# Attention into a squared-ReLU layer on one core: M's tiled matmuls regrouped with the second scores, and the last output tile moved behind tile 34

## The chip, the cores and the metric

The kernel runs on one core of a Trainium2 chip. The metric is device time in microseconds (us) of one execution. Engines are called PE (TensorE, matmuls), DVE (VectorE), ACT (ScalarE), POOL (GpSimd) and SP (SyncE); the last two mostly issue DMAs here. PSUM has eight banks, in which PE leaves its results and from which DVE and ACT copy them out.

## The reference

Eight batches of eight heads, 576 tokens of 64 numbers, and 32 packed queries `p` per head. Two attentions in a row, and then a layer with a squared ReLU over all 4608 tokens:

```python
def sm_attn(qq, kk, vv):
    s = scale * np.matmul(qq, kk.transpose(0, 1, 3, 2))
    s = s - np.max(s, axis=-1, keepdims=True)
    a = np.exp(s)
    a = a / (np.sum(a, axis=-1, keepdims=True) + 1e-09)
    return np.matmul(a, vv)
p_packed = sm_attn(p, k, v)
out = sm_attn(q, p_packed, p_packed)
x = out.transpose(0, 2, 1, 3).reshape(4608, 512)
h = x @ w_in                       # 512 x 2048
r = np.maximum(h, 0.0)
return (r * r) @ w_out             # 2048 x 512
```

## The kernel before, in words

Each batch goes through a chain of steps, and the steps of several batches are woven into one another.

- **Loads.** POOL issues all DMAs for q, k, v and the weights, at most eight in flight, in one order (`Lk`, `Lq`, `Lv`, `LWI` for w_in, `LWO` for w_out).
- **Tk, Tq.** DVE transposes k and q.
- **S1, SX, E.** First scores of `p` against k: PE (`s1`, `s1_both`), maximum on DVE, exponential on ACT, norm on DVE, then PE turns the weights (`s1_tr`) and ACT or DVE copies them out as `e1`.
- **PV, XT.** `pv_both` gives the packed values; `pp_turn` and `spread` on PE and small copies bring them into `ppT` and into the blocks `pq_bd`.
- **S2, C, N.** Second scores of q against the packed values (`s2_both`): 32 matmuls on tiles of 64 x 32 of the array, eight of which run side by side. DVE turns the result out of PSUM (`s2_turn`, three pieces), then maximum, subtraction, exponential (ACT), sum, multiplication and a last turn (`n_turn`) into `a2`.
- **M.** Instead of multiplying the attention weights by the packed values and then by w_in, the kernel first makes M, packed values times w_in: 128 x 2 x 2048 per batch, in four quarters `c` of 512 columns. A quarter is eight matmuls of 64 x 32 tiles with 512 columns (`m`) into two banks. The quarters are copied out either as one wide copy of 1024 columns (`m_out`, where the two banks are a pair) or as two narrow ones (`m_half`).
- **F1.** `f1_mm`: M times `a2`, 16 blocks of 128 rows per batch, each four matmuls of 288 columns into a pair of banks, ReLU on ACT, square on DVE into `gT`.
- **F2.** For each of 36 tiles of 128 tokens, 16 matmuls of 512 columns (`f2_mm`, `gT` times `w_out_b`) into one bank, a copy to `o_sb` and four stores on SP's queue (`store`). The last tile, 35, goes in three pieces of 256, 128 and 128 output columns (`fz_steps`, `fz_mm`), named F2.35, F2.36 and F2.37; each is copied and stored half by SP and half by ACT's queue.

Banks 0 to 3 are the two pairs `HB`, 4 and 5 are `AB`, 6 and 7 are `OB`. F1 takes a pair, F2 a bank of `OB`; scores and M (`mode=2`) take a pair and banks 4 and 5.

The order is made before the program is recorded. `Plan` holds streams of `Step`s; a step has pieces with an engine, a planned duration, banks, and the steps that must be done before it. `forward` goes through planned time and gives each free engine the ready piece with the lowest priority number; the priorities are a base level per kind of step plus the numbers of `TABLE`. A change of `mode` on PE costs `TURN` in the plan. Each engine then works through its own instructions strictly in that order and waits on semaphores. Where the plan leaves PE a gap before the first F2, dummy matmuls on zeros (`keep_clock`) are put in.

The three tiled runs of a batch are these steps before: `S2.b.0` (second scores), `M.b.0` (quarters 0 and 1) and `M.b.2` (quarters 2 and 3):

```python
return [Step(f"M.{b}.{c}", [[[("PE", 0.48, lambda c=c: mm(c))]], outs(c)], [f"XT.{b}/3.0"] + pre(c),
             banks=[x + (4, 5) for x in HB], free=[(1, None)], mode=2) for c in (0, 2)]
```

Of the kernel before, what the change touches and what calls it, by code (L numbers as in the profile page):

```python
# [8 lines left out]
ACT = mybir.ActivationFunctionType  # L9
# [5 lines left out]
P = 128  # L15
# [38 lines left out]
class Plan:  # L54
# [193 lines left out]
TABLE = {'o': {'P.0': -17.44, 'X.0': -515.84, 'P.2': -467.13, 'X.1': -217.88, 'La0': -1045.51, 'La1': -646.79,  # L248
# [47 lines left out]


def kernel_impl(tc, q, k, v, p, w_in, w_out, out):
# [17 lines left out]
    FUSE = ()  # L316
# [3 lines left out]
    with ExitStack() as ctx:  # L320
# [591 lines left out]
        def s1_steps(b):  # L912
            after = [f"X.{min(b // 2, 1)}"] + ([f"PV.{b - 1}.{qd}" for qd in QDS if b == 1 or qd == 0] if b else []) + gate(b, 1)
# [21 lines left out]
        def pv_steps(b):  # L935
# [14 lines left out]
            return [Step(nm, [[[("PE", 0.41, lambda: T[b].pv_both(U[nm]))]]],  # L950
# [9 lines left out]
        def m_steps(b):  # L960
# [19 lines left out]
            def first():  # L980
                T[b].s2_rest(U[f"S2.{b}.1"])
                mm(0)

            def pre(c):
                return [f"LWI.{x}.{i}" for x in (c, c + 1) for i in range(2)] + ([f1n(b - 2, NFB - 1)] if b > 1 else [])
            if b not in FUSE:
                return [Step(f"M.{b}.{c}", [[[("PE", 0.48, lambda c=c: mm(c))]], outs(c)], [f"XT.{b}/3.0"] + pre(c),
                             banks=[x + (4, 5) for x in HB], free=[(1, None)], mode=2) for c in (0, 2)]
            return [Step(f"S2.{b}.1", [NO], [f"XT.{b}"] + [f"Tq.{b}.{qd}" for qd in QDS] + [f"N.{b - 1}.{qd}" for qd in QDS], banks=HB),
                    Step(f"M.{b}.0", [[[("PE", 0.58, first)]]], [f"S2.{b}.1"] + pre(0), banks=[x + (4, 5) for x in HB], mode=2),  # L990
                    Step(f"MX.{b}.0", [NO, outs(0)], [f"M.{b}.0"], free=[(1, f"M.{b}.0")]),
                    Step(f"M.{b}.2", [[[("PE", 0.48, lambda: mm(2))]], outs(2)], [f"XT.{b}/3.0"] + pre(2),
                         banks=[x + (4, 5) for x in HB], free=[(1, None)], mode=2)]

        def m_of(b, fb):
            c = fb * FB // WCH
            return [f"M.{b}.{c}.{x}" for x in QDS] if b in SOLO else [f"{'MX' if b in FUSE and c < 2 else 'M'}.{b}.{c // 2 * 2}"]

        def s2_steps(b):
# [30 lines left out]
            if b in TURNED:  # L1030
                turns = [[("DVE", 0.7 if x == 0 else 0.38, lambda x=x: T[b].s2_turn(x))] for x in range(3)]
                return [Step(nm, [[[("PE", 0.55, lambda: T[b].s2_both(U[nm]))]], turns] + front(4, 1152), pre,
                             banks=[x + (4, 5) for x in HB], free=[(1, None)], mode=2), Step(f"C.{b}", chain(4, 1152), [nm])] + [
                        Step(f"N.{b}.{x}", [[[("DVE", 0.7, lambda x=x: T[b].n_turn(x))]]], [f"C.{b}"] + ([f1n(b - 2, NFB - 1)] if b > 1 else [])) for x in range(2)]
# [175 lines left out]
```

## Time and profile before

| | us |
|---|---|
| median of 3 runs | 250.99 |
| lowest, highest | 250.13, 252.03 |
| the profiled execution | 250.5 |
| its span | 248.7 |
| PE, DVE, ACT, POOL busy in the span | 237.6, 186.9, 168.3, 42.9 |
| granted clock of PE | 0.999 of full |

The span goes from the first to the last instruction that the profiler saw; 1.8 us of the execution's time lie around it. Busy times are sums of the instructions of an engine, and matmuls overlap one another, so the start of one matmul to the start of the next says more than the length of a row. The largest groups are F2 (line 831, 544 matmuls of 512 columns, 138.2 us) and F1 (line 775, 448 matmuls, 70.4 us); M (line 589) has 256 matmuls and the second scores of batches 1 to 7 (line 622) 224. DMA queue 0, which POOL feeds, moves 18.55 MB, and the DMA engines are busy in slices 1 to 16 of 40 and nearly idle afterwards.

### The profile page before, as it was taken

What the parts mean: (1) busy time and instruction counts of PE and PEld (TensorE: products, weight loads), DVE (VectorE), ACT (ScalarE), POOL (GpSimd) and SP (SyncE); (2) the same over time, 40 slices, a digit from 0 to 9 for tenths busy, and PEclk for the clock granted to TensorE, in tenths of its full rate; (3) what the DMA queues carried; (4) which work ended last, traced back from release to release, by engine and by line L of the source; (5) the groups of instructions that cost most, each with busy time, mean ns of one, the idle gap of its engine ahead of it and who ended that gap; (6) DMA issues with size and microseconds to landing.
All of it is one profiled execution on the core that took longest, in us unless ns stands there. A gap on an engine that the chain in (4) does not pass through costs nothing.

```text
span 248.7 us, 5896 instructions
## 1 busy us (share of the span) xinstructions
PE 237.6 (96%) x2352; PEld 130.5 (52%) x2352; DVE 186.9 (75%) x356; ACT 168.3 (68%) x302; POOL 42.9 (17%) x76
## 2 busy tenths in 40 slices
PE   7788899899999999999999999999999999999992
PEld 5464464356534755465536654465444764466641
DVE  5678988997699779956996789946999758765100
ACT  8547899968828868787767855799045883997010
POOL 8745545433334320000000000000000000000000
PEclk9999999999999999999999999999999999999999
DMA  6999999999999999640022103110223101301222
GB/s 111 197 192 207 205 201 203 202 231 240 219 229 221 233 218 221 112 99 22 23 63 65 45 3 83 46 44 3 77 56 81 44 1 42 86 1 42 76 78 60
DMA packets 26715, 28.50 MB, mean 115 GB/s; under 512 B 5440, under 2 KB 18112, under 8 KB 26688
## 3 DMA queue, kind: packets, MB, share of 16 engines
q0 software_dynamic: 18960, 18.55, 45.7%
q1 hardware_dynamic: 6960, 9.32, 13.7%
q8 instruction: 18, 0.29, 0.4%
q10 hardware_dynamic: 768, 0.26, 0.4%
q14 instruction: 9, 0.07, 0.1%
HBM read 37.22 MB, written 9.44 MB: 188 GB/s over the span
## 4 chain that ended last, share of the span: by engine, by line
PE 77%; DMA 16%; POOL 2%; ACT 1%; issue 1%; DVE 0%; DVEq 0%; ACTq 0%; POOLq 0%
PE pb L831 45%; PE ps L775 22%; DMA w_in_b<-in_moe_w_in_dram 8%; DMA w_out_b<-in_moe_w_out_dram 4%; DMA q_b<-in_q_dram 4%; PE ps L589 2%; PE ps L475 2%; PE pb L848 1%; PE pb L500 1%; PE ps L622 1%; PE pb L589 1%; PE pb L514 1%; ACT r L813 1%; POOL k_b L416 0%; POOL q_b L416 0%
## 5 line engine op out<-in xcount | busy, mean ns | idle before, releaser
L831 PE MATMUL pb<-w_out_b,gT 128*128 128x512 bf16 x544 | 138.2, 380 | 0.7 <-DMA w_out_b<-in_moe_w_out_dram 0.6
L831 PEld LDWEIGHTS <-gT 128*128 128x128 bf16 x560 | 51.6, 98 | 59.1 <-issue 8.2
L813 ACT ACTIVATE r<-ps 128x576 bf16<-128x576 f32 x112 | 70.8, 655 | 13.7 <-PE ps L775 10.1
L775 PE MATMUL ps<-a,M 128*128 128x288 bf16 x448 | 70.4, 286 | 0.1
L823 DVE TENSOR_TENSOR gT<-r 128x576 bf16<-128x576 bf16 x112 | 49.7, 455 | 26.5 <-ACT r L813 25.4
L775 PEld LDWEIGHTS <-M 128*128 128x128 bf16 x448 | 42.9, 98 | 20.5 <-issue 1.3
L366 ACT COPY o_sb<-pb 128x512 f32<-128x512 f32 (+1 forms) x18 | 10.3, 571 | 23.8 <-PE pb L831 19.8
L368 DVE COPY o_sb<-pb 128x512 f32<-128x512 f32 (+2 forms) x19 | 12.1, 638 | 14.5 <-PE pb L848 12.8
L487 ACT ACTIVATE e1x<-ps,n 128x576 bf16<-128x576 f32 x16 | 11.8, 743 | 12.9 <-DVE n L483 12.9
L734 ACT ACTIVATE e<-d 128x1152 bf16<-128x1152 f32 (+2 forms) x9 | 9.1, 1008 | 12.9 <-DVE d L729 12.9
L366 ACT CAST M<-pb 128x512 bf16<-128x512 f32 x30 | 16.5, 600 | 1.3 <-PE pb L589 1.3
L366 ACT CAST M<-ps 128x1024 bf16<-128x1024 f32 (+1 forms) x15 | 14.7, 980 | 3.8 <-PE ps L589 3.8
L451 DVE STREAM_TRANSPOSE kT<-k_b 128x576 f32<-128x576 f32 x16 | 12.0, 764 | 2.9 <-DMA k_b<-in_k_dram 2.9
L421 POOL DMA_DIRECT2D v_b<-in_v_dram x16 | 11.2, 700 | 12.9 <-DMA k_b<-in_k_dram 6.2
L416 POOL DMA_DIRECT2D q_b<-in_q_dram x16 | 8.9, 559 | 24.7 <-DVE kT L451 13.9
L352 PE MATMUL pb<-zero 128*128 128x256 bf16 x72 | 11.9, 317 | 1.1 <-DVE zero L371 1.1
L483 DVE TENSOR_REDUCE n<-ps 128x1 f32<-128x576 f32 x16 | 11.6, 749 | 1.0 <-PE ps L475 0.8
L740 DVE TENSOR_REDUCE t<-e 128x36 f32<-128x1152 bf16 (+2 forms) x9 | 10.3, 1141 | 1.6 <-ACT e L734 1.5
L416 POOL DMA_DIRECT2D k_b<-in_k_dram x16 | 8.7, 544 | 13.7 <-DMA q_b<-in_q_dram 3.6
L366 ACT COPY e<-pb 128x640 bf16<-128x640 bf16 x14 | 9.5, 699 | 1.9 <-PE pb L500 1.9
L444 DVE STREAM_TRANSPOSE qT<-q_b 128x576 f32<-128x576 f32 x14 | 10.3, 755 | 0.4 <-DMA q_b<-in_q_dram 0.4
L746 DVE TENSOR_TENSOR n<-e,r 128x1152 bf16<-128x1152 bf16 (+2 forms) x9 | 10.4, 1160 | 0.2
(103 smaller groups left out, 239.2 us busy)
## 6 DMA issues: line engine op xcount, KB each, us to landing
out_dram<-o_sb SPq DMA_DIRECT2D x141, 64.0 KB, 1.7
k_b<-in_k_dram POOLq DMA_DIRECT2D x16, 288.0 KB, 11.7
q_b<-in_q_dram POOLq DMA_DIRECT2D x16, 288.0 KB, 11.9
v_b<-in_v_dram POOLq DMA_DIRECT2D x8, 320.0 KB, 12.3
v_b<-in_v_dram POOLq DMA_DIRECT2D x8, 256.0 KB, 11.7
w_in_b<-in_moe_w_in_dram POOLq DMA_DIRECT2D x8, 256.0 KB, 10.6
w_out_b<-in_moe_w_out_dram POOLq DMA_DIRECT2D x8, 256.0 KB, 10.5
p_b<-in_p_dram POOLq DMA_DIRECT2D x1, 192.0 KB, 10.6
```

The source lines that it names most:

```text
L352: nc.tensor.matmul(half(7)[:, :2 * P], lhsT=zero[:, :P], rhs=zero, start=True, stop=True)
L366: nc.scalar.copy(dst, src)
L368: eng.tensor_copy(dst, src)
L416: nc.gpsimd.dma_start(t, src[self.b, qd * QH:(qd + 1) * QH].rearrange("h (a j) d -> (h a) (j d)", j=JT))
L421: nc.gpsimd.dma_start(self.v[64 * i:64 * i + 64, :, :n * D], src[:, :, i * GM * D:(i * GM + n) * D])
L451: nc.vector.transpose(kT[:, qd].rearrange("p s x -> p (s x)").bitcast(F32).rearrange("p (x a j2) -> p j2 x a", a=32, j2=2), self.t.k[qd][: ...
L483: nc.vector.tensor_reduce(self.n1[:, qd:qd + 1], self.ps1[qd], axis=AX.X, op=ALU.max, negate=True)
L487: nc.scalar.activation(e1x[:, qd], self.ps1[qd], ACT.Exp, bias=self.n1[:, qd:qd + 1], accum_out=self.d1[:, qd:qd + 1])
L775: nc.tensor.matmul(ps[:, c], lhsT=a.M[:, qd, fb * FB:(fb + 1) * FB], rhs=a.a2[:, qd, c * HALF:(c + 1) * HALF], start=(qd == 0), stop=(qd = ...
L813: nc.scalar.activation(dst, src, ACT.Relu)
L823: eng.tensor_tensor(out=Att.cols(gT[:, fb, o:o + S]), in0=r, in1=r, op=ALU.mult)
L831: nc.tensor.matmul(po[t], lhsT=gT[:, fb, n0:n0 + P], rhs=w_out_b[:, fb, :], start=(fb == 0), stop=(fb == NFB - 1))
```

## The change

For batches 2 to 7 (`FUSE`) the second scores and quarter 0 of M become one run of tiled matmuls (32 + 8), and quarters 1, 2 and 3 another (24). For that, scores take a second pair of banks (`SH`), and the second run likewise (`MH`). Quarters 0, 1 and 2 are copied out wide (`MX`, `MY` and the first of `MZ`), quarter 3 in two narrow copies. The next batch's first scores are put behind the second run. The three pieces of tile 35 now stand in the stream of even tiles, the first behind tile 34, which has moved to the other stream; each further piece waits for the one before it as far as its last matmul. `TABLE` has new numbers throughout, so the whole order is new: among other things the spread of `p` for batches 0 and 1 (`X.0`) goes from ACT to DVE, and two pairs of w_out blocks change places in POOL's queue. The computation is the same. `FUSE` was empty before, so the parts for `b in FUSE` were not in use.

```diff
-TABLE = {...
+TABLE = {...
...
-    FUSE = ()
+    FUSE = range(2, 8)
...
         def s1_steps(b):
-            after = [f"X.{min(b // 2, 1)}"] + ([f"PV.{b - 1}.{qd}" for qd in QDS if b == 1 or qd == 0] if b else []) + gate(b, 1)
+            after = [f"X.{min(b // 2, 1)}"] + ([f"PV.{b - 1}.{qd}" for qd in QDS if b == 1 or qd == 0] if b else []) + ([f"M.{b - 1}.1"] if b - 1 in FUSE else []) + gate(b, 1)
...
-            return [Step(f"S2.{b}.1", [NO], [f"XT.{b}"] + [f"Tq.{b}.{qd}" for qd in QDS] + [f"N.{b - 1}.{qd}" for qd in QDS], banks=HB),
-                    Step(f"M.{b}.0", [[[("PE", 0.58, first)]]], [f"S2.{b}.1"] + pre(0), banks=[x + (4, 5) for x in HB], mode=2),
-                    Step(f"MX.{b}.0", [NO, outs(0)], [f"M.{b}.0"], free=[(1, f"M.{b}.0")]),
-                    Step(f"M.{b}.2", [[[("PE", 0.48, lambda: mm(2))]], outs(2)], [f"XT.{b}/3.0"] + pre(2),
-                         banks=[x + (4, 5) for x in HB], free=[(1, None)], mode=2)]
+            full = lambda c: [[("ACT", 0.91, lambda: T[b].m_out(c, A)), ("DVE", 1.14, lambda: T[b].m_out(c, V))]]
+
+            def rest():
+                T[b].m(1, U[f"MH.{b}"])
+                T[b].m(2, U[f"M.{b}.1"])
+                T[b].m(3, U[f"M.{b}.1"], 2)
+            return [Step(f"MX.{b}", [NO, full(0)], [f"S2.{b}.0"], free=[(1, f"SH.{b}")]),
+                    Step(f"MH.{b}", [NO], [f"S2.{b}.0"] + pre(2), banks=HB),
+                    Step(f"M.{b}.1", [[[("PE", 0.7, rest)]]], [f"MH.{b}"], banks=[x + (4, 5) for x in HB], mode=2),
+                    Step(f"MY.{b}", [NO, full(1)], [f"M.{b}.1"], free=[(1, f"MH.{b}")]),
+                    Step(f"MZ.{b}", [NO, outs(2)], [f"M.{b}.1"], free=[(1, f"M.{b}.1")])]
...
+                def scores():
+                    T[b].s2_both(U[nm])
+                    T[b].m(0, U[f"SH.{b}"])
+                return [Step(f"SH.{b}", [NO], pre + [f"LWI.0.{i}" for i in range(2)] + ([f1n(b - 2, NFB - 1)] if b > 1 else []), banks=HB),
+                        Step(nm, [[[("PE", 0.79, scores)]]], [f"SH.{b}"], banks=[x + (4, 5) for x in HB], mode=2),
+                        Step(f"ST.{b}", [NO, turns] + front(4, 1152), [nm], free=[(1, nm)])] + rest
...
         def fz_steps(t, h):
-                        + ([f"F2.{k - 1}.{fb}"] if h else []), banks=OB + AB if fb == 0 else ()) for fb in range(last)]
+                        + ([] if h else [f"F2.{NT - 2}.{last - 1}"]), banks=OB + AB if fb == 0 else ()) for fb in range(last)]
...
-                               [f1n(b, last), f"LWO.{last // 2}"] + ([f"F2.{k - 1}.{last}"] if h else []), [] if h else [("osb", 1)], [] if h else [("osb", 2, None)],
+                               [f1n(b, last), f"LWO.{last // 2}"] + ([f"F2.{k - 1}.{last}/1.0"] if h else []), [] if h else [("osb", 1)], [] if h else [("osb", 2, None)],
...
-        plan.stream(sum([f2_steps(t) for t in range(0, NT, 2) if t != 2], []))
-        plan.stream(sum([f2_steps(t) for t in range(1, NT - 1, 2) if t != 3] + [fz_steps(NT - 1, h) for h in range(len(FZ))], []))
+        plan.stream(sum([f2_steps(t) for t in range(0, NT - 2, 2) if t != 2] + [fz_steps(NT - 1, h) for h in range(len(FZ))], []))
+        plan.stream(sum([f2_steps(t) for t in (1, *range(5, NT - 1, 2), NT - 2)], []))
```

On PE the order of the end was tile 33, pieces F2.35 and most of F2.36, tile 32, tile 34, piece F2.37; it is now tiles 31, 32, 33, 34 and then F2.35, F2.36, F2.37 without a break. Of M's 30 copies in batches 2 to 7 two, both wide, go to DVE (batches 2 and 5); the others stay on ACT. The copies of `e1` of batches 4 and 6 go from ACT to DVE. Between a batch's first and second tiled run stand 8, 16, 17, 18, 12 and 33 F2 matmuls (batches 2 to 7), and between its second run and the next batch's first scores 10, 20, 21, 16 and 22.

More of the change, by code (lines that the diff above doesn't have):

```diff
@@ L245, in use @@
         self.wait, self.margin = z.get("w", 0.0), z.get("m", 0.0)
-TABLE = {'o': {'P.0': -17.44, 'X.0': -515.84, 'P.2': -467.13, 'X.1': -217.88, 'La0': -1045.51, 'La1': -646.79,
[47 rows of a table removed]
+TABLE = {'o': {'P.0': 12.64, 'X.0': -182.5, 'P.2': 786.53, 'X.1': 824.47, 'La0': -989.93, 'La1': -654.2, 'La2':
[54 rows of a table added]
 def kernel_impl(tc, q, k, v, p, w_in, w_out, out):
@@ L949, in pv_steps @@
                 return res
-            return [Step(nm, [[[("PE", 0.41, lambda: T[b].pv_both(U[nm]))]]],
+            return [Step(nm, [[[("PE", 0.33, lambda: T[b].pv_both(U[nm]))]]],
                          [f"E.{b}.{qd}" for qd in QDS] + [f"Lv.{b}.0", f"Lv.{b}.1", "I2"], (), [("vb", 0, f"Lv.{b}.0")], banks=AB, mode=3),
@@ L978, in mm @@
                 T[b].m(c + 1, U[f"M.{b}.{c}"], 2)
-            def first():
-                T[b].s2_rest(U[f"S2.{b}.1"])
-                mm(0)
             def pre(c):
@@ L988, in m_steps @@
                              banks=[x + (4, 5) for x in HB], free=[(1, None)], mode=2) for c in (0, 2)]
-            return [Step(f"S2.{b}.1", [NO], [f"XT.{b}"] + [f"Tq.{b}.{qd}" for qd in QDS] + [f"N.{b - 1}.{qd}" for qd in QDS], banks=HB),
-                    Step(f"M.{b}.0", [[[("PE", 0.58, first)]]], [f"S2.{b}.1"] + pre(0), banks=[x + (4, 5) for x in HB], mode=2),
-                    Step(f"MX.{b}.0", [NO, outs(0)], [f"M.{b}.0"], free=[(1, f"M.{b}.0")]),
-                    Step(f"M.{b}.2", [[[("PE", 0.48, lambda: mm(2))]], outs(2)], [f"XT.{b}/3.0"] + pre(2),
-                         banks=[x + (4, 5) for x in HB], free=[(1, None)], mode=2)]
+            full = lambda c: [[("ACT", 0.91, lambda: T[b].m_out(c, A)), ("DVE", 1.14, lambda: T[b].m_out(c, V))]]
[8 more added lines that the diff above has]
+                    Step(f"MZ.{b}", [NO, outs(2)], [f"M.{b}.1"], free=[(1, f"M.{b}.1")])]
         def m_of(b, fb):
             c = fb * FB // WCH
-            return [f"M.{b}.{c}.{x}" for x in QDS] if b in SOLO else [f"{'MX' if b in FUSE and c < 2 else 'M'}.{b}.{c // 2 * 2}"]
+            return [f"M.{b}.{c}.{x}" for x in QDS] if b in SOLO else [(f"MX.{b}", f"MY.{b}", f"MZ.{b}", f"MZ.{b}")[c] if b in FUSE else f"M.{b}.{c // 2 * 2}"]
         def s2_steps(b):
@@ L1031, in s2_steps @@
                 turns = [[("DVE", 0.7 if x == 0 else 0.38, lambda x=x: T[b].s2_turn(x))] for x in range(3)]
-                return [Step(nm, [[[("PE", 0.55, lambda: T[b].s2_both(U[nm]))]], turns] + front(4, 1152), pre,
-                             banks=[x + (4, 5) for x in HB], free=[(1, None)], mode=2), Step(f"C.{b}", chain(4, 1152), [nm])] + [
-                        Step(f"N.{b}.{x}", [[[("DVE", 0.7, lambda x=x: T[b].n_turn(x))]]], [f"C.{b}"] + ([f1n(b - 2, NFB - 1)] if b > 1 else [])) for x in range(2)]
+                rest = [Step(f"C.{b}", chain(4, 1152), [f"ST.{b}" if b in FUSE else nm])] + [
+                    Step(f"N.{b}.{x}", [[[("DVE", 0.7, lambda x=x: T[b].n_turn(x))]]], [f"C.{b}"] + ([f1n(b - 2, NFB - 1)] if b > 1 else [])) for x in range(2)]
+                if b not in FUSE:
+                    return [Step(nm, [[[("PE", 0.55, lambda: T[b].s2_both(U[nm]))]], turns] + front(4, 1152), pre,
+                                 banks=[x + (4, 5) for x in HB], free=[(1, None)], mode=2)] + rest
+                def scores():
[4 more added lines that the diff above has]
+                        Step(f"ST.{b}", [NO, turns] + front(4, 1152), [nm], free=[(1, nm)])] + rest
             return [Step(nm, [a] + front(3, 1024), pre, banks=HB, free=[(2, None)]),
@@ L1110, in kernel_impl @@
         setup()
-        plan.levels.update(L=-99, I=-99, LP=-99, I2=5, P=-9, X=-8, G=0, T=0, S1=1, SX=1, E=1, PV=1, XT=1, S2=2, SA=2, SB=2.5, SC=2.6, TR=2.3, C=2, N=2, M=3, MX=3, SR=2, FA=14, F1=15, F2=30)
+        plan.levels.update(L=-99, I=-99, LP=-99, I2=5, P=-9, X=-8, G=0, T=0, S1=1, SX=1, E=1, PV=1, XT=1, S2=2, SA=2, SB=2.5, SC=2.6, TR=2.3, C=2, N=2, M=3, MX=3, MY=3, MZ=3, MH=3, SH=2, ST=2, SR=2, FA=14, F1=15, F2=30)
         plan.stream([Step("P.0", [[[("DVE", 0.2, lambda: nc.vector.tensor_copy(p_b[:, :2 * NQD], p_f))]],
```

101 rows, old and new, of the table TABLE are left out of this document.

## The prediction

> **What bounds the kernel now.** I read the page first, then busy time by stretch, then the waits of TensorE (PE) in the start, then the timeline around one batch and around the end.
>
> ```profile
> span 248.7 us, 5896 instructions
> PE 237.6 (96%) x2352; PEld 130.5 (52%) x2352; DVE 186.9 (75%) x356; ACT 168.3 (68%) x302; POOL 42.9 (17%) x76
> ...
> PE   7788899899999999999999999999999999999992
> ...
> DMA  6999999999999999640022103110223101301222
> ```
>
> From slice 10 on PE is full; before that the DMA row is full and PE is not. By stretch (us, then PE, PEld, DVE, ACT, POOL busy with counts, clock, DMA share):
>
> ```profile
> 54.00:244.00 190.00, 189.81 (x1865) 103.55 (x1863) 142.28 (x264) 126.63 (x222) 13.74 (x23) 1.00 0.45 94
> ```
>
> For 190 us PE leaves 0.19 us empty at full granted clock, DVE and ACT a quarter to a third. What shortens this stretch is only less PE time. The start is another matter; PE's waits between 20 and 56 us:
>
> ```profile
> PE ps L788 <- DVE a L368: 0.7, 1, 0.7
> PE pb L831 <- DMA w_out_b<-in_moe_w_out_dram: 0.6, 1, 0.6
> PE ps L460 <- DVE kT L451: 0.6, 1, 0.6
> ```
>
> The second is the last block of w_out: F2's matmul on its rows 14 and 15 of tile 0 starts at 48.22 when that load lands, 0.6 us after PE was ready.
>
> One batch of the full stretch (batch 7), PE alone, start and length:
>
> ```profile
> 206.31 5.35 PE L831 MATMUL pb<-w_out_b,gT 128*128 128x512 bf16 x24
> 211.59 0.41 PE L589 MATMUL ps<-w_in_b,ppT 64*32 64x512 bf16 x8
> 211.82 0.40 PE L589 MATMUL pb<-w_in_b,ppT 64*32 64x512 bf16 x8
> 212.15 2.76 PE L831 MATMUL pb<-w_out_b,gT 128*128 128x512 bf16 x12
> 214.84 0.41 PE L589 MATMUL ps<-w_in_b,ppT 64*32 64x512 bf16 x8
> ```
>
> The first eight tiled M matmuls and the next eight start 0.23 apart, and F2 follows 0.33 later: a run of 16 holds PE 0.56 (211.59 to 212.15). F2 itself goes at 0.2155 each (24 from 228.11 to 233.29), so 12 would take 2.59, but 212.15 to 214.84 is 2.69: entering a tiled run costs 0.10 more. The end:
>
> ```profile
> 242.84 1.06 PE L848 MATMUL pb<-w_out_b,gT 128*128 128x128 bf16 x16
> 243.04 0.59 ACT L366 COPY o_sb<-pb 128x512 f32<-128x512 f32 x1 [2.87 <-PE pb L831]
> 243.65 1.96 SPq L842 DMA_DIRECT2D out_dram<-o_sb  x4
> 244.00 0.29 DVE L368 COPY o_sb<-pb 128x128 f32<-128x128 f32 x1 [8.34 <-PE pb L848]
> 244.33 0.55 ACTq L854 DMA_DIRECT2D out_dram<-o_sb  x1
> 245.71 0.54 SPq L854 DMA_DIRECT2D out_dram<-o_sb  x1
> ```
>
> The last piece is copied at 244.29, but SP's half of its store waits until 245.71 behind four stores of tile 34. The span ends 3.0 after that issue.
>
> **The change, part by part.**
>
> *Merging tiled runs (batches 2 to 7).* Before, a batch has three tiled runs with F2 between them: scores (32 matmuls, 205.66 to 206.31, 0.65), M 16, M 16. After: scores with 8 of M, then M 24. No matmul of the computation is removed; two dummy ones (L352) fall away, both ahead of the stretch. One run of 16 costs 0.56 + 0.10 = 0.66; its 16 matmuls appended to runs that are open anyway cost two groups of eight, 2 x 0.22 = 0.44. That is 0.22 a batch, 1.3 us for six. Bounds: 0 if the appended groups cost as much as a run of their own, 1.4 if each costs no more than one F2 matmul, 0.2155, which has as many columns. I take 1.3, since scores and M stand in the same 64*32 form in the rows and groups inside a run are seen 0.22 to 0.23 apart. No run of before has M directly behind scores. For that case the Trainium skill ("TensorEngine Tiling (Array Packing)", Key Properties) says that changing the tiling mode drains TensorE and moving between tiles of one mode does not; no trace here can show it yet, and by it this term would be the same 1.3.
>
> *What the merged runs hold.* Scores now keep two pairs of banks and banks 4 and 5, as M's second run does; F1 and the next batch's scores need a pair. So from scores to M's last wide copy only F2 can run, and its matmuls are the cover. Batch 2 has the least: 8 F2 between the runs, 10 after. First gap: DVE turns the scores out (after batch 7's: from 206.62, 0.96 after scores began, to 208.12, so 1.5); needed 2.46 after scores begin. M's third group, which uses those banks, comes at 0.87 + 8 x 0.2155 + 0.10 + 0.44 = 3.1. Slack 0.7. M's first group needs a wide copy by ACT (1.01, L366) that starts about 1.1 after scores begin: 2.1, against 2.7. Second gap: DVE's maximum (1.34, L721) stands ahead of its wide M copy (never on DVE before; twice the 0.69 row, 1.38): 2.46 + 1.34 + 1.38 = 5.2. The scores of batch 3 come at 2.7 + 0.78 + 10 x 0.2155 + 0.10 = 5.7. Slack 0.5. The other batches have 12 to 33 F2 in the first gap and 14 to 22 in the second, 2.6 us and more. Cost 0; bounds -0.2 (the 0.19 that is empty now) to +1.5 (half of these twelve gaps late by 0.25).
>
> *Copies.* A batch's M goes out in three wide and two narrow copies (3 x 1.01 + 2 x 0.60 = 4.2) in place of two and four (4.4). Two wide ones and four 0.70 copies of e (L366) go from ACT to DVE: 4.8 us more on ACT's idle side, about 4.7 on DVE, which has 48 us free in the stretch. Cost 0; without that cover, the late gaps above.
>
> *New order, start.* Load order on POOL is the same up to two swaps among w_out blocks; the last w_out block keeps its place, so it lands as now, at 48.2. From that matmul to the first F1 of batch 1 (53.7) the two orders have the same PE work. Start changes ahead of 48.2 (the spread of p to DVE, which waits 1.33 for k anyway; second-half tokens of batch 0 before batch 1's scores; less M of batch 0 on DVE) end in that wait. Cost 0; bounds 0 to +0.6, if PE arrives later than its 0.6 of slack, by up to as much again.
>
> *The last tile behind tile 34.* SP's queue now has tiles 31, 32, 33, 34 and then the pieces. A tile's four stores take SP 1.96; tiles end 10 or 16 F2 apart, 2.2 or 3.4, so SP never piles up. Count from tile 34's last matmul: copied at 1.01 (as now, 242.62 to 243.63), SP stores 1.03 to 2.99. Pieces' last matmuls at 1.87, 2.81 and 3.69 (0.11 each for the 256 wide, 0.055 for the 128 wide). First piece: copied by DVE at 2.6; ACT issues its half to 3.3 (0.65), SP's half 2.99 to 3.64. Second: now on ACT, copied 3.4 to 3.67, issues on both until 4.25. Third: ready 3.97, but its copy is on ACT too and waits: 4.35 to 4.62, both issues at 4.65, 0.96 after the last matmul. Now the last issue is 245.71 - 243.68 = 2.03 after it, so 1.07 is won; ACT's half lands later than SP's (2.0 and 1.8 us in the issues), which takes 0.2 back. I take -0.9; bounds 0 and -1.4 (copy not held by ACT). F2 of tile 31 needs the last square of F1: 229.46, 1.35 after F1's last matmul at 228.11; 7 F2 (1.51) cover it in place of 8.
>
> *Sum.* -1.3 - 0.9 + 0 + 0 = -2.2. The profiled execution took 250.5 (span 248.7 and 1.8 around it): 248.3. The median of the runs shown is 250.99, 0.5 above it, and they spread over 1.9; I put the base in between, at 250.7, and the time at 248.5; the cases below have the same base.
>
> **Rivals.**
>
> *The appended groups cost full runs.* For it: M behind scores is in no row. Against: equal form, and 0.22 between groups. Then only the end remains: 249.8.
>
> *The start loses its pin.* For it: PE had three waits of 0.6 to 0.7 on DVE and DMA there, and the new order changes all three; DVE is busy 27.5 of 31 us between 23 and 54. Against: 0.6 of slack. A loss of 1.2 beyond that: 249.7.
>
> *Slower: copies out of PSUM become the bound.* Place: the gap between M's second run and the next scores. If in each batch a wide copy (1.38) more stood ahead of the release than I see, 1.38 - 0.5 of slack, 0.9, would be PE idle six times: +5.4, and with the -2.2 that is 253.9. It decides from 0.5 us lateness on. For it: only F2 may run there, and DVE has maxima and subtractions of 1.35 in the queue. Against: five of the six batches have more than batch 2's cover, and ACT is lighter. By itself: the Trainium skill, same page, PSUM Bottleneck, warns that faster tiled matmuls leave evacuation of PSUM as the limit; whether that holds here is this rival.
>
> **How the numbers follow.** Forecast 0.74, the full runs 0.10, lost pin 0.09, copies 0.07. A measurement of this kernel tells about 1% (2.5 us) from no change; 1% below 250.99 is 248.48, so half of the forecast lies beyond: faster 0.37. The other half and the two middle rivals: same 0.56. Slower 0.07. The forecast's own range is 247.7 (every good bound: -1.4 - 0.2 - 1.4) to 249.5 (1.0 of the bad ones). To hold eight in ten I reach past the two middle rivals and add half a microsecond at each end for the spread of the runs: 247.2 to 250.4.
>
> **What would show it.** Right: two tiled runs per batch from batch 2 on, 0.87 and 0.78 long; the first F1 of batch 1 still near 53.7; PE again full from 54 to some 242.4; last store issue about 1 us after the last matmul. Wrong: scores with M at 1.2 or more, the first F1 past 54.3, L475 or L589 with waits on ACT or DVE of over 0.5 each, or SP issuing past 244.5.

## The result and the profile after

The changed kernel takes 249.62 us in the median of 22 runs (248.91 to 251.02), the kernel before 250.61 on the same chip (22 runs, 249.85 to 252.03). The ratio is 0.9961, 95% interval 0.9948 to 0.9974: 1.0 us less. 2.2 less was forecast; the time lies inside the range.

The profiled execution of the changed kernel took 249.95 us, its span is 248.2. Its page, busy times and PE's row of the 40 slices (35 of the 2350 matmul records are missing in this trace, so PE's sum is low; a second profile of the same kernel has all of them and 236.9):

```profile
span 248.2 us, 5863 instructions
PE 234.0 (94%) x2315; PEld 129.9 (52%) x2350; DVE 193.1 (78%) x368; ACT 163.5 (66%) x284; POOL 43.0 (17%) x76
...
PE   7789799899999999999999999999999999999992
```

PE is still full from slice 10 to the last. So I cut the span at two points that both traces show, the first F1 of batch 1 and the last matmul, and the end once more at the last store's issue and at its landing (us):

| | first F1 | from there to the last matmul | last issue behind it | landing behind the issue | to the end | the end in all |
|---|---|---|---|---|---|---|
| before | 53.71 | 189.97 | 2.03 | 1.82 | 1.20 | 5.05 |
| after | 54.15 | 189.30 | 1.32 | 2.07 | 1.33 | 4.73 |

0.67 comes from the full stretch and 0.32 from the end, 1.0 together, which is the difference of the medians. The 0.44 at the start is not of the change (below).

The tiled runs came out as the prediction has them. Batch 2 on PE, start, length and count (scores began at 68.55):

```profile
69.08 0.41 PE L596 MATMUL ps<-w_in_b,ppT 64*32 64x512 bf16 x8
69.42 1.90 PE L838 MATMUL pb<-w_out_b,gT 128*128 128x512 bf16 x7
71.25 0.63 PE L596 MATMUL ps<-w_in_b,ppT 64*32 64x512 bf16 x16
71.69 0.40 PE L596 MATMUL pb<-w_in_b,ppT 64*32 64x512 bf16 x8
72.02 2.33 PE L838 MATMUL pb<-w_out_b,gT 128*128 128x512 bf16 x10
```

Scores with a quarter of M hold PE from 68.55 to 69.42, 0.87, and the three other quarters from 71.25 to 72.02, 0.77. Forecast were 0.87 and 0.78. (Of the eight F2 between them one record is missing.) But PE now has waits in the full stretch. Who waits for whom, us in total, times, longest (the same view of the kernel before has no line between 54 and 244):

```profile
PE pb L838 <- issue: 0.6, 4, 0.2
PE pb L838 <- DVE gT L830: 0.3, 2, 0.2
PE ps L782 <- ACT r L820: 0.2, 1, 0.2
```

Only the third line is a wait. The first two are six places where the trace lacks a matmul (two weight loads and one matmul stand there); in the second profile, which has all of them, the third line stands alone. But this view leaves out what is under 0.15 and counts from the modelled end of a matmul, so I compared the starts of all matmuls with the usual distance of their kind. That gives three larger places, here in the timeline of all engines, with the lines between left out; the bracket gives the idle time ahead and who ended it:

```profile
163.74 0.77 DVE L451 STREAM_TRANSPOSE qT<-q_b 128x576 f32<-128x576 f32 x1
164.43 0.42 DVE L830 TENSOR_TENSOR gT<-r 128x576 bf16<-128x576 bf16 x1
164.90 0.10 PEld L838 LDWEIGHTS <-gT 128*128 128x128 bf16 x1 [0.37 <-DVE gT L830]
...
171.66 0.26 ACT L373 COPY ppT<-pb 128x128 bf16<-128x128 bf16 x1
172.21 1.19 ACT L820 ACTIVATE r<-ps 128x576 bf16<-128x576 f32 x2 [0.29 <-ACT ppT L373]
172.91 0.65 PE L782 MATMUL ps<-a,M 128*128 128x288 bf16 x4 [0.16 <-ACT r L820]
...
204.64 0.58 DVE L375 CAST pq_bd<-pb 32x128 bf16<-32x128 f32 x2
205.31 0.53 ACT L373 CAST pq_bd<-pb 32x128 bf16<-32x128 f32 x2 [0.38 <-DVE pq_bd L375]
205.59 0.09 PEld L629 LDWEIGHTS <-pq_bd 64*32 64x32 bf16 x2 [0.42 <-DVE pq_bd L375]
```

At 164.56 + 0.12 (the last F1 matmul ahead of it and its usual length) an F2 matmul is ready; its square of F1 stands on DVE behind a transpose of q, and PE loses 0.23. At 172.38 + 0.22 an F1 matmul is ready, but its banks come free only with a ReLU that ACT starts at 172.21, behind a small copy and 0.29 in which ACT does nothing: PE loses 0.32. At batch 7 the four copies that make `pq_bd` are split over two engines. ACT's two wait for a semaphore that DVE's second one sets, an order that the program asks for, and all scores but the first matmul come 0.30 late (205.59, then 205.89). The scores of batches 5 and 6 lose 0.12 and 0.09 in the same way: there DVE makes all four copies, and the last ends at 150.09 and 178.52, just after the scores have begun at 150.02 and 178.49. These new waits make 1.06. The kernel before had two of its own, 0.25 at 200.79 (F1) and 0.09 at 56, which are gone. By this list the net is +0.7; by difference it is 0.5 to 0.6 (six merges at 0.2 and the measured -0.67), so the list and the difference agree to within 0.2. The second profile shows the same five waits, 1.05 in sum.

The end, ACT's and SP's lines:

```profile
242.43 0.65 ACTq L861 DMA_DIRECT2D out_dram<-o_sb  x1
242.60 2.70 SPq L861 DMA_DIRECT2D out_dram<-o_sb  x3
243.57 0.27 ACT L373 COPY o_sb<-pb 128x128 f32<-128x128 f32 x1 [2.81 <-DMA out_dram<-o_sb]
243.86 0.57 ACTq L861 DMA_DIRECT2D out_dram<-o_sb  x1
244.48 0.27 ACT L373 COPY o_sb<-pb 128x128 f32<-128x128 f32 x1 [0.65 <-ACT o_sb L373]
244.77 0.56 ACTq L861 DMA_DIRECT2D out_dram<-o_sb  x1
```

The last matmul starts at 243.45. ACT issues piece 1 until 243.09, but copies piece 2, whose matmuls have been done since 242.8, only at 243.57; everything behind it is late by as much.

### The profile page after: what moved, and what is told of

Same layout as the page of the kernel before. It is cut to its first block, busy times and chain, and to the rows that moved or that the text cites. A ratio compares the mean times of both kernels' runs of the same rounds, so it can differ in the third digit from the quotient of the medians.

```text
span 248.2 us, 5863 instructions
## 1 busy us (share of the span) xinstructions
PE 234.0 (94%) x2315; PEld 129.9 (52%) x2350; DVE 193.1 (78%) x368; ACT 163.5 (66%) x284; POOL 43.0 (17%) x76
## 4 chain that ended last, share of the span: by engine, by line
PE 71%; DMA 17%; DVE 4%; issue 2%; POOL 2%; ACT 2%; SPq 0%; ACTq 0%; DVEq 0%; POOLq 0%
PE pb L838 41%; PE ps L782 21%; DMA w_in_b<-in_moe_w_in_dram 8%; DMA q_b<-in_q_dram 4%; DMA w_out_b<-in_moe_w_out_dram 4%; PE ps L596 2%; PE ps L482 1%; PE pb L507 1%; PE ps L629 1%; ACT r L820 1%; PE pb L521 1%; PE pb L629 1%; DMA out_dram<-o_sb 1%; DVE gT L830 1%; DVE n L753 1%
## 5 line engine op out<-in xcount | busy, mean ns | idle before, releaser
L838 PE MATMUL pb<-w_out_b,gT 128*128 128x512 bf16 x509 | 133.5, 379 | 3.1 <-issue 0.8
L820 ACT ACTIVATE r<-ps 128x576 bf16<-128x576 f32 x112 | 71.9, 654 | 14.9 <-PE ps L782 10.3
L782 PE MATMUL ps<-a,M 128*128 128x288 bf16 x448 | 71.8, 286 | 0.4 <-ACT r L820 0.2
L830 DVE TENSOR_TENSOR gT<-r 128x576 bf16<-128x576 bf16 x112 | 50.8, 456 | 25.8 <-ACT r L820 24.7
L373 ACT COPY o_sb<-pb 128x512 f32<-128x512 f32 (+1 forms) x20 | 11.0, 555 | 24.0 <-PE pb L838 20.4
L373 ACT CAST M<-ps 128x1024 bf16<-128x1024 f32 (+1 forms) x20 | 19.2, 969 | 10.2 <-PE ps L596 10.1
L375 DVE COPY o_sb<-pb 128x512 f32<-128x512 f32 (+1 forms) x17 | 11.3, 662 | 10.8 <-PE pb L855 10.2
L373 ACT CAST M<-pb 128x512 bf16<-128x512 f32 x18 | 9.9, 596 | 1.3 <-PE pb L596 1.3
L645 DVE STREAM_TRANSPOSE a<-n 128x576 bf16<-128x576 bf16 (+1 forms) x14 | 10.1, 743 | 0.1
```

The costliest lines, as they stand in the source:

```text
L373: nc.scalar.copy(dst, src)
L375: eng.tensor_copy(dst, src)
L782: nc.tensor.matmul(ps[:, c], lhsT=a.M[:, qd, fb * FB:(fb + 1) * FB], rhs=a.a2[:, qd, c * HALF:(c + 1) * HALF], start=(qd == 0), stop=(qd = ...
L820: nc.scalar.activation(dst, src, ACT.Relu)
L830: eng.tensor_tensor(out=Att.cols(gT[:, fb, o:o + S]), in0=r, in1=r, op=ALU.mult)
L838: nc.tensor.matmul(po[t], lhsT=gT[:, fb, n0:n0 + P], rhs=w_out_b[:, fb, :], start=(fb == 0), stop=(fb == NFB - 1))
```

## The experiments

All are one kernel with a few instructions moved; the rest keeps its order. Ratios are to the kernel before, run on the same chip beside it; the other columns are of each one's profile.

| run | median | ratio, 95% interval | first F1 | to the last matmul | the end |
|---|---|---|---|---|---|
| after | 249.62 | 0.9961 (0.9948, 0.9974) | 54.15 | 189.30 | 4.73 |
| three tiled runs | 250.77 | 1.0007 (0.9994, 1.0020) | 53.83 | 190.46 | 4.73 |
| four tiled runs | 252.40 | 1.0070 (1.0049, 1.0091) | 53.59 | 191.84 | 4.71 |
| old end on after | 250.11 | 0.9977 (0.9966, 0.9988) | 53.98 | 189.31 | 5.01 |
| new end on before | 249.79 | 0.9968 (0.9956, 0.9980) | 53.44 | 189.95 | 4.39 |
| pieces on DVE | 249.51 | 0.9946 (0.9929, 0.9963) | 54.41 | 189.34 | 4.37 |
| two waits | 249.35 | 0.9946 (0.9933, 0.9959) | 53.97 | 189.06 | 4.51 |
| six more on ACT | 249.23 | 0.9939 (0.9925, 0.9954) | 53.43 | 189.00 | 4.41 |
| two more on ACT | 249.56 | 0.9959 (0.9946, 0.9972) | 54.03 | 189.02 | 4.71 |
| one load less | 249.02 | 0.9934 (0.9921, 0.9947) | 53.13 | 189.30 | 4.73 |
| all together | 248.49 | 0.9914 (0.9901, 0.9928) | 53.24 | 189.09 | 3.90 |
| before, one run | 250.65 | | 53.85 | 189.94 | 5.05 |
| after, one run | 249.06 | | 53.27 | 189.30 | 4.72 |

### What the merge is worth: three and four tiled runs

```diff
                 def scores():
                     T[b].s2_both(U[nm])
-                    T[b].m(0, U[f"SH.{b}"])
+                    late[:] = [lambda: T[b].m(0, U[f"SH.{b}"])]
...
+        def behind(p):      # called behind each recorded piece
+            if late and p.alts[p.alt][0] == "PE" and p.step.name[:2] == "F2":
+                late.pop()()
```

> The changed kernel, with quarter 0 of M taken out of the scores' run again and put one F2 matmul further back, so that batches 2 to 7 have three tiled runs (32, 8 and 24 matmuls). All else keeps its order. Theory (a run's entering and leaving costs 0.22 us, so the merge was worth six of them): 6 x 0.22 = 1.3 us slower than the changed kernel's 249.6, about 250.9, level with the kernel before. Rival (the merge itself gave only the 0.7 by which the full stretch became shorter, and the new waits of PE are no cost of their own): 0.7 slower, about 250.3.

For four runs, the second run as well:

```diff
                 T[b].m(1, U[f"MH.{b}"])
-                T[b].m(2, U[f"M.{b}.1"])
-                T[b].m(3, U[f"M.{b}.1"], 2)
+                late[:] = [lambda: (T[b].m(2, U[f"M.{b}.1"]), T[b].m(3, U[f"M.{b}.1"], 2))]
```

> As the run with three tiled runs, and the second run is split too: quarter 1 of M, one F2 matmul, quarters 2 and 3. Batches 2 to 7 then have four tiled runs (32, 8, 8 and 16). Theory: twelve more entries and leavings than the changed kernel at 0.22, 2.6 us slower, about 252.2, slower than the kernel before by 1.6. Rival (0.12 a run): 1.4 slower, about 251.0.

The full stretch grew from 189.30 to 190.46 with six runs more and to 191.84 with twelve: 0.19 and 0.21 a run. The medians grew by 1.15 and 2.78. The rivals (0.12 a run) fall. So the merge is worth 1.2 to 1.3, as the prediction's term of 1.3 says, and the kernel with three runs is level with the kernel before: all else in the change, the new end too, gave nothing in sum.

### What the end is worth: old end on after, new end on before

```diff
+        def patch(rows):    # after planning: these tiles' matmuls in this order
+            ... for t in (35, 36, 34, 37):   # on before: (32, 34, 35, 36, 37)
+                ... copies and stores keep their distance from the tile's last matmul
```

> The changed kernel with the end of the kernel before: pieces 1 and 2 of tile 35 ahead of tile 34, piece 3 behind it and copied by DVE. Theory (the new end is worth only what the two traces differ by behind the last matmul, 5.04 against 4.73): 0.3 slower than the changed kernel, about 249.9; the last store is issued 2.0 us after the last matmul. Rival (the sum of the prediction, 0.9, is right for the end, and something else ate it): 0.9 slower, about 250.5.

> The kernel before with the end of the changed one: tiles 31, 33, 32, 34 and then the three pieces of tile 35, piece 3 copied by ACT. Nothing else is moved. Theory: 0.3 faster than the kernel before, last issue 1.3 us after the last matmul, piece 2's copy on ACT starting about 0.45 after ACT's issue of piece 1 ended. Rival (prediction): 0.9 faster, last issue 1.0 after the last matmul. Its start is that of the kernel before: if the first F1 of batch 1 comes later than 53.9 here too, the 0.44 us by which it came later in the changed kernel's profile is a difference between executions and not of the order.

The old end costs the changed kernel 0.28 behind the last matmul (4.73 to 5.01), as the theory says; the ratio makes it 0.4. The new end on the kernel before is where the theory fell: the end shrank by 0.66 (5.05 to 4.39), the median by 0.8, near the prediction's 0.9. The instructions of the end are the same as in the changed kernel. The difference is one pause of ACT:

```profile
243.22 0.27 ACT L366 COPY o_sb<-pb 128x128 f32<-128x128 f32 x1 [2.53 <-PE pb L848]
...
244.42 0.57 ACTq L854 DMA_DIRECT2D out_dram<-o_sb  x1
```

ACT's issue of piece 1 ended at 243.03 here, and the copy follows after 0.19; in the changed kernel it took 0.48 (243.09 to 243.57). The last issue is 1.03 behind the last matmul (243.39); the prediction had 0.96.

### A pause that belongs to the place in ACT's stream: six more, two more

I numbered all rows of ACT in the traces in order of start, from 0, semaphore rows too, and looked at row 447:

| kernel | row 447 is | idle ahead of it | the same step elsewhere |
|---|---|---|---|
| before | second semaphore row of a copy | 0.33 | 0.04 |
| after, three runs, four runs | piece 2's copy | 0.33 | 0.04 |
| old end on after | a semaphore row of tile 34's copy | 0.34 | 0.04 |
| pieces on DVE | semaphore row of the last issue | 0.33 | 0.04 |

0.29 is lost there whatever stands in the row. The changed kernel has one more, 128 rows ahead: row 319 is the ReLU at 172.21.

```diff
-            nc.vector.memset(zero, 0.0)
+            nc.vector.memset(zero, 0.0), [nc.scalar.copy(junk[:, i:i + 1], zero[:, :1]) for i in range(6)]
```

> The changed kernel with six copies of one column on ACT at the very start, where ACT is idle; they write a tile that nobody reads. All else is as it was. In the changed kernel's profile ACT stands still for 0.29 with its semaphores met at two rows, number 319 (the ReLU at 172.21, for which PE then waits 0.32) and number 447 (piece 2's copy at 243.57), 128 rows apart; row 447 is 0.29 late in the profile of the kernel before too, where nobody waits for it. Theory (the pause belongs to the place in ACT's stream): six rows on, both pauses fall where ACT is idle or a long instruction runs; PE's wait at 172.38 and 0.29 of the end go, 0.5 to 0.6 faster, about 249.0. Rival (the pause belongs to these instructions): no change, 249.6.

> As the run with six small copies on ACT at the start, but with two. Theory (ACT pauses 0.29 at row 319 and row 447 of its stream, whatever stands there): row 447 is now the semaphore row right behind ACT's first issue of tile 35, where the pause still delays piece 2's copy, so the end stays at 4.73 behind the last matmul; row 319 is now the copy of ppT, whose pause runs while the ReLU ahead of it is still at work, so PE's wait at 172.38 goes. 0.3 faster than the changed kernel, all of it between the first F1 and the last matmul (189.0). Rival (any added rows help both, or the gain had another cause): both places change, or neither.

With six more rows the ReLU follows the copy of ppT at once and the end moves up; ACT's line at 171, then the end:

```profile
170.92 0.26 ACT L373 COPY ppT<-pb 128x128 bf16<-128x128 bf16 x1
171.19 2.10 ACT L820 ACTIVATE r<-ps 128x576 bf16<-128x576 f32 x3
...
242.27 0.27 ACT L373 COPY o_sb<-pb 128x128 f32<-128x128 f32 x1 [2.52 <-PE pb L855]
...
243.16 0.27 ACT L373 COPY o_sb<-pb 128x128 f32<-128x128 f32 x1 [0.63 <-PE pb L855]
243.46 0.56 ACTq L861 DMA_DIRECT2D out_dram<-o_sb  x1
```

Stretch 189.00 (0.30 less), last issue 1.02 behind the last matmul (0.30 less), ratio 0.9939: both halves of the theory, from six copies that compute nothing. With two more rows only the first half came: 189.02, and the end at 4.71; row 447 was then the semaphore row behind piece 1's issue and 0.33 late. So the rival falls, by the profile: the 0.28 won in the stretch is too little for the times, whose ratio of 0.9959 does not differ from the changed kernel's beyond the intervals. What ACT does in that time the traces do not say: an 8 KB packet of a DMA queue of the kind "instruction" starts 0.66 and 0.84 us behind the two pauses of the changed kernel, which fits a fetch of instructions but does not show it.

### Pieces 2 and 3 copied by DVE

```diff
+                if p.stage == 1 and p.step.name in ("F2.36.15", "F2.37.15"):
+                    p.alt = 1       # DVE in place of ACT
```

> The changed kernel with pieces 2 and 3 of tile 35 copied out by DVE in place of ACT, which then only issues DMAs there. Theory (the end is long because ACT, between its two issues, first goes through four semaphores of old stores and then pauses, so piece 2's copy starts at 243.57 and piece 3's behind ACT's second issue at 244.48): copies at about 242.8 and 243.7, last issue about 0.7 after the last matmul in place of 1.32, so 0.6 faster than the changed kernel, about 249.0. Rival (the last landing is set by something else than the last issue): no change, 249.6.

```profile
242.73 2.27 ACTq L861 DMA_DIRECT2D out_dram<-o_sb  x3
...
243.18 0.29 DVE L375 COPY o_sb<-pb 128x128 f32<-128x128 f32 x1 [0.48 <-PE pb L855]
244.00 0.29 DVE L375 COPY o_sb<-pb 128x128 f32<-128x128 f32 x1 [0.53 <-PE pb L855]
```

The last issue came 0.69 behind the last matmul (243.75), as expected. But it landed 2.35 behind its issue in place of 2.07, so 0.36 of the 0.63 is left, and the ratio agrees (0.4 less than the changed kernel). SP's half, issued at 244.41, took 2.19 in place of 1.81. Why both halves take longer to land here is open.

### Two waits taken away

```diff
+                if p.step.name == "XT.6" and p.stage == 3:
+                    p.alt = 0       # copy of ppT on DVE
+                if p.step.name == "F1.5.0" and p.stage == 2:
+                    p.start = next(x.start for x in rows if x.step.name == "Tq.6.0") - 0.001
```

> The changed kernel with two single moves behind 160 us: the first square of F1 of batch 5 goes ahead of the transpose of q of batch 6 on DVE (an F2 matmul waited 0.23 for it at 164.56), and the copy of ppT of batch 6 goes from ACT to DVE (an F1 matmul waited 0.32 for ACT's ReLU at 172.38). Theory (PE is full in this stretch, so every wait of PE is the kernel's time): 0.4 to 0.55 faster than the changed kernel, about 249.1, and from the first F1 to the last matmul 188.8 in place of 189.3. Rival (the next dependence takes their place): no change, 189.3.

189.06 in place of 188.8: one half worked, one was displaced. The ReLU is on time and its wait of 0.32 gone. The square is early too, but the transpose that it passed now stands ahead of a copy out of PSUM, and F2 waits for that:

```profile
164.86 0.65 DVE L375 COPY o_sb<-pb 128x512 f32<-128x512 f32 x1
...
165.56 0.38 PE L838 MATMUL pb<-w_out_b,gT 128*128 128x512 bf16 x1 [0.22 <-DVE o_sb L375]
```

That F2 was ready at 165.18 and lost 0.38, more than the 0.23 won. And the end became shorter by 0.22 though nothing was done there: ACT has two rows less, so row 447 is now the issue of piece 2 and the pause lies mostly behind the copy ahead of it.

### What holds the start

This run leaves out one of the eight loads of w_out (0.25 MB), so that its output is not the layer's; the work of PE stays the same.

```diff
         def dma_w_out(c):
+            if c == 3:
+                return
...
-                             rhs=w_out_b[:, fb, :]
+                             rhs=w_out_b[:, fb - 2 if fb in (6, 7) else fb, :]
```

> The changed kernel without the load of rows 6 and 7 of w_out (0.25 MB); F2 reads rows 4 and 5 a second time in their place. Theory (the first F1 of batch 1 is held by the load queue, through the last w_out rows and k of batch 2): all later loads land 1.2 us earlier, PE's wait of 0.6 for w_out goes, and the first F1 of batch 1 comes at 53.3 in place of 53.6 to 54.2; 0.6 faster, about 249.0. Rival (DVE's chain up to the last turn of a2 holds it just as well): 0 to 0.2 faster.

> The kernel before once more, for a second look at its start. Two profiles with its start had the first F1 of batch 1 at 53.71 and 53.44. Theory (the start differs from execution to execution with the first loads and not between the kernels): anywhere from 53.3 to 54.4, and ACT's row 447 late by 0.29 again.

> The changed kernel once more. Seven profiles with its start had the first F1 of batch 1 at 53.4 to 54.4, mean 53.9. Theory: within the same bounds; 189.3 from there to the last matmul, 4.73 from the last matmul to the end, ACT's rows 319 and 447 late by 0.29 again.

With one load less the first F1 came at 53.13, earlier than in any of the thirteen other profiles, and the time fell by 0.6 to 0.7 against the changed kernel. Its stretch and its end are those of the changed kernel (189.30 and 4.73), so all of that lies in the start, and the load queue does hold it. How, the profiles show: in twelve of the thirteen others the first F1 comes 5.48 to 5.52 behind the F2 matmul that waits for the last block of w_out, whichever kernel it is. With one load less PE waits at 48.94 for another thing, a copy of `o_sb` by ACT that frees a bank, and from there runs without a break to the first F1, 4.19 later:

```profile
48.94 1.24 PE L840 MATMUL pb<-w_out_b,gT 128*128 128x512 bf16 x5 [0.40 <-ACT o_sb L373]
```

In "two waits", the thirteenth, it is this copy too (49.78, and the first F1 4.19 later). In the profiles with the start of the kernel before the first F1 came at 53.44, 53.71 and 53.85 (mean 53.67), in the ten with the new start between 53.24 and 54.41 (mean 53.79). Kernels with the same start differ by over 1 us, the two means by 0.12.

### All together

The two moves of "two waits", pieces on DVE and six more on ACT, and piece 3 stored by SP alone:

```diff
-            out = [[("SP", ...)], [("ACT", ...)]]
+            out = [[("SP", ...)], [("ACT", ...)]][:1 if h == 2 else 2]
...
+            n = 2 if h == 2 else 1
-            eng.dma_start(dst, ob[t][64 * x:64 * x + 64, FZ[h]])
+            eng.dma_start(dst, ob[t][64 * x:64 * x + 64 * n, FZ[h]])
```

> All that helped, together, on the changed kernel: the two moves behind 160 us, pieces 2 and 3 of tile 35 copied by DVE, the six small copies on ACT at the start, and piece 3 stored by SP alone in one DMA (halves issued by ACT landed 2.1 us after the issue, by SP 1.8). Theory: 0.5 from the waits of PE in the full stretch (188.8 in place of 189.3) and 1.0 from the end (last issue 0.65 after the last matmul, landing 1.85 later, so 3.7 from the last matmul to the end in place of 4.73): about 248.1, 2.5 faster than the kernel before. Rival (the gains overlap, or one DMA of double size lands later by as much as ACT's half did): 248.7.

248.49, 0.9914 (0.9901 to 0.9928) of the kernel before, the fastest of all: 2.2 us less, as much as was forecast for the change alone. The end is 3.90 (issue at 0.67, landing 1.97 behind it). The stretch, 189.09, is longer than with six more copies alone (189.00): the displaced wait at 165 is in it.

## Why the prediction was wrong in size

- **What bounds the kernel: right.** PE is full for 189 us, and every PE wait that was added or removed in it (three and four runs, six more) showed in the time.
- **Merging tiled runs, -1.3: right.** 0.19 to 0.21 a run by two doses against 0.22. M directly behind scores starts no new run: the first eight M matmuls behind scores hold PE 0.34 (69.08 to 69.42), the 0.33 that the prediction saw for a last group in an open run. The trace so agrees with the Trainium skill ("TensorEngine Tiling (Array Packing)", Key Properties), by which a change of tiling mode drains TensorE and a mere change of tile does not.
- **What the merged runs hold, and the copies, both 0: the step that failed.** Measured +0.5 to +0.7. The twelve gaps that I counted held: no wait for the wide copies of M or for the turned scores. I looked for a late copy only where the diff adds one. But `TABLE` is new, so every small copy and square has a new place, and two kinds stood wrong: a transpose ahead of a square (0.23), and the copies of `pq_bd`, which end just behind the start of the scores of batches 5, 6 and 7 (0.12, 0.09 and 0.30; at batch 7 five F2 cover four copies). The fifth wait, 0.32, is ACT's pause at row 319, which falls on a ReLU here; with six or two more rows the copy of ppT stands ahead of that ReLU as before, and PE does not wait. Free time of ACT and DVE in the sum (48 us on DVE) was no cover: what counts is the 0.2 to 0.7 us at each place. The upper bound of +1.5 held it, but I took 0, near the good bound.
- **The end, -0.9: mis-sized at one step, -0.32 measured.** The count from tile 34's last matmul (239.76) has piece 2's copy at 3.4; it came at 3.81. 0.29 of it is ACT's pause at row 447, the rest four semaphores of old stores that ACT goes through first. From there every number is late by 0.4 and the last issue at 5.01 in place of 4.65. ACT's half landing 0.2 later was right (2.07 against 1.82). 0.12 more goes at the very end: SP closes by going through its queues' semaphores in a fixed order, 0.06 each, and the one that lands last now stands two places further ahead in that order. On the kernel before, whose pause falls elsewhere, the same end gave 0.66 to 0.8, so the mechanism was right.
- **The start, 0: right,** and for the reason given: the first F1 follows the landing of the last w_out block by the same 5.5 in both kernels. Close behind that wait stands the next one, ACT's copy of `o_sb`, which holds the start where w_out lands early. The 0.44 between the two profiles lies in when that block lands (48.22 and 48.67).
- **Rivals.** The appended groups do not cost full runs (four runs refutes it), the start keeps its pin, and copies of M out of PSUM are no bound: the waits of 0.1 to 0.3 are single places, not one per batch.
- **Marks.** Right: the lengths of the runs. Wrong: first F1 at 54.15 (but inside the spread), PE full until 243.45 in place of 242.4, last issue 1.32 in place of about 1. One of the signs of being wrong came, SP issuing past 244.5 (its last at 244.77, in a profile whose first F1 is 0.44 later); the others did not.

So of the missing 1.2 us, 0.6 is one mechanism, ACT's pause at two bad places. The rest is, in the stretch, the wait of 0.23 behind the transpose and the 0.51 of the scores of batches 5 to 7, less the 0.34 that the old order had, and in the end the semaphores ahead of piece 2's copy and at SP's close, some 0.1 each. Taking away the 0.23 only displaced it; whether the scores' waits go with more cover was not tried, so their cause rests on the traces alone.

## What to carry to other kernels

Price a merge of tiled runs by the run that falls away, not by its matmuls, and test it with two doses. When an order is made anew, a gain of 1 us on a full engine is easily half eaten by waits of 0.2 to 0.3 us at places that the diff does not name, so bound them from zero upwards and not around zero. And where an engine stands still with its semaphores met, count its rows before you explain the instruction: moving the stream by a few idle instructions is a cheap test.

## What the hardware showed that I had not expected

- ACT loses 0.29 us at a fixed row of its stream (447, seen in twelve of the fourteen profiles, and 319 in the changed kernel), whatever instruction is there; if a long instruction runs ahead of it or the engine is idle, nobody waits for it. Six idle copies, which make it fall there, won 0.6 us.
- The last store half, issued by ACT, landed 2.07 behind its issue in the changed kernel; SP's 1.82 in the kernel before; SP's one DMA of double size 1.97. Where DVE copied the pieces, the halves took 2.35 (ACT) and 2.19 (SP).
